# Where the layer norm's rows are kept between the norm and its transposition

## The chip, the core and the metric

The kernel runs on one core of one Trainium2 chip. A core has five engines that run their own instruction queues in order: TensorE (PE; its weight loads are shown apart as PEld), VectorE (DVE), ScalarE (ACT), GpSimd (POOL) and SyncE (SP), which here issues the DMA transfers. They wait for one another by semaphores. The metric is the device time of one execution in microseconds, the median of the runs.

## The reference, cut

Four batches of 768 tokens and 384 features pass through a gated linear attention scan, a Fourier mixer with a layer norm and an MLP, and a second mixer with an MLP over tokens and one over features.

```python
for t in range(S):                      # attention, per head, S = 768
    S_re, S_im = ar * S_re - ai * S_im + kv, ar * S_im + ai * S_re
    y[:, :, t] = np.einsum('bhd,bhde->bhe', q[:, :, t], S_re)
...
X = np.fft.fft(np.fft.fft(x, axis=1), axis=2)
u = x + np.real(X)
mu, var = mean(u), mean((u - mu) ** 2)
un = (u - mu) / np.sqrt(var + 1e-06)    # the layer norm
x = u + np.maximum(un @ w_ch1, 0.0) @ w_ch2
...
u = x + (np.maximum(x.T @ w_tok1, 0.0) @ w_tok2).T
out = u + np.maximum(u @ w_ch1, 0.0) @ w_ch2
```

## The kernel before

Work comes in two streams. The **chain** of a batch is stage 1 (a scan over 48 steps on DVE with its preparation on ACT and POOL, whose results PE transposes into a tile `qkt`, L642, and then eight chunks of attention: scores L753, L768/L769, outputs L802/L808) and stage 2 (the Fourier mixer: sums on DVE and POOL, L982, L988, L999; products L1022 and L1033; joins L1085 that give six tiles `u`; statistics L1092/L1093; the norm, L1112 on ACT and L1114 on DVE). The **dense** stream of a batch is a token mixing (L1147, L1165) between two MLPs (L926 into the hidden layer, L942 out of it). A dense product is a matmul of 128x128 by 128x384; they come in groups of nine that share a PSUM tile `l` of three, and each group ends in a DVE or ACT instruction that empties it (L930/L932 for `h`, L945 for `u`). Each layer works in quarters: 54 products of L926, then 54 of L942.

The chain of batch b+1 runs while the dense stream of batch b is worked off. Instructions get a priority from their stream and their place in the program, and a scheduler with a timeline of its own writes each engine's queue from it before the kernel runs; the order on the chip is then fixed. On PE the chain has priority over dense products, on DVE and ACT dense work has priority.

`transposed` (L900 to L911) takes the six normalized tiles in the order 0, 3, 1, 4, 2, 5: three transpositions on PE each (L906), a copy to `th` on ACT (L909) and the rest to `tl` on DVE (L910). `th` and `tl` are the inputs of the first MLP. Tiles come from pools: tag `qk` has one buffer of 12,288 words, used in turn as `qkt` in stage 1 and as the workspace `ws` in stage 2, with the layout `WSP`; tag `P` has two buffers of 384 words, used by `V` (L741), the values of an attention chunk. A tile's buffer is given to the next tile of its tag when all readers are done. The normalized rows `un` are the words 6176 to 8480 of `ws`, so that the next batch's `qkt` can't be written before L906 has read them.

A handover, below, is the place where the norm of a batch ends and its dense stream may begin. The first is that of batch 0, the fourth that of batch 3, after which only dense work is left. The last stage is stage 2 of batch 3.

Of the kernel before, what the change touches and what calls it, by code (L numbers as in the profile page):

```python
# [12 lines left out]
ACTF = mybir.ActivationFunctionType  # L13
ALU = mybir.AluOpType
# [22 lines left out]
OFF = ((2, 3), 1, 0)  # L37
# [16 lines left out]
def attn_fft_mixer_kernel(ctx: ExitStack, tc: tile.TileContext, aL, xL, vL, wL, qN, kN, vN, arN, aiN,  # L54
# [18 lines left out]
    ve, se, ge = Prio(nc.vector, "v"), Prio(nc.scalar, "v"), Prio(nc.gpsimd, "v")  # L73
# [11 lines left out]
    def shaped(v, shape):  # L85
        if len(shape) == 3:
            return v.rearrange("p (a b) -> p a b", b=shape[2])
        if len(shape) == 4:
            return v.rearrange("p (a b c) -> p a b c", b=shape[2], c=shape[3])
        return v  # L90

    def alloc(tag, shape, dt=F32, name=None):
        n = 1
        for x in shape[1:]:
            n *= x
        t = pool.tile([128, SIZE[tag]], dt, tag=tag, bufs=BUFS[tag], name=name or tag)
        return shaped(t[0:shape[0], 0:n], shape)
# [3 lines left out]
    def palloc(tag, shape):  # L101
        n = 1
        for s in shape[1:]:
            n *= s
        t = psum.tile([128, 512], F32, tag=tag, bufs=PSB[tag], name=tag)
        v = t[0:shape[0], 0:n]
        if len(shape) == 3:
            v = v.rearrange("p (a b) -> p a b", b=shape[2])
        return v

    def r32(ap):
        return ap.bitcast(F32)
# [46 lines left out]
    LAST = [None]  # L159
# [739 lines left out]
    def transposed(u, un, pt):  # L899
        th = [alloc("T", [128, 3, 384], F32R, name="th") for _ in range(2)]  # L900
        tl = [alloc("T", [128, 3, 384], F32R, name="tl") for _ in range(2)]
        for i in range(6) if un is None else (0, 3, 1, 4, 2, 5):
            src = u[i] if un is None else un[:, i, :]
            px = palloc(pt, [128, 3, 128])
            for dt in range(3):
                te.transpose(px[:, dt, :], src[:, dt * 128:dt * 128 + 128], ident)  # L906
            o = (i % 3) * 128
            hi = th[i // 3][:, :, o:o + 128]
            se.copy(out=hi, in_=px)  # L909
            ve.tensor_tensor(out=tl[i // 3][:, :, o:o + 128], in0=px, in1=r32(hi), op=ALU.subtract)  # L910
        return th, tl  # L911

    def mlp(u, b, p0, th, tl, done):
        for qd in range(4):
# [33 lines left out]


    WSP = {"xf": (0, 3072), "Z": (0, 1552), "xr": (1552, 1536), "fd": (3088, 3088), "cb": (3088, 1737),  # L950
           "xd": (6176, 3072), "un": (6176, 2304), "smat": (9248, 2048), "cc": (4825, 1158)}
    ZK = ((128, 64), (128, 64), (128, 65), (128, 63))

    def stage2(b):
        space = alloc("qk", [128, 12288], name="ws")
        def part(name, pat=None, **kw):
            o, n = WSP[name]
            v = space[:, o:o + n]
            return v.rearrange(pat, **kw) if pat else v

        smat = part("smat", "p (t k j) -> p t k j", t=4, k=2)
        sp.dma_start(out=smat, in_=cS)
        u = [alloc("u", [128, 384], name=f"u{i}") for i in range(6)]


        if b == 0:

            xm, xp = (alloc("h", [112, 4, 384], name="xf") for _ in range(2))
            xd = alloc("h", [112, 4, 384], name="xd")
            xd = [[xd[:, 0:2], xd[:, 2:4]], [alloc("tmp", [112, 2, 384], name="xd") for _ in range(2)]]  # L970
        else:
            xf = part("xf", "p (a b) -> p a b", a=8)[0:112]
            xm, xp = xf[:, 0:4, :], xf[:, 4:8, :]
            xd = part("xd", "p (s r a b) -> p s r a b", s=2, r=2, a=2)[0:112]
            xd = [[xd[:, s, r] for r in range(2)] for s in range(2)]
# [54 lines left out]
        def smm(o, ty, j0, first, last, extra=False):  # L1030
            for kt in range(2):
                kk = ZK[ty][kt]
                te.matmul(out=o, lhsT=smat[0:kk, ty, kt, j0:j0 + 128], rhs=Z[0:kk, 2 * ty + kt, 0:193],  # L1033
                          start=(first and kt == 0), stop=(last and kt == 1))
                if extra and kt == 0:
                    for k2 in range(2):
                        kk = ZK[2][k2]
                        te.matmul(out=o[0:1], lhsT=fk[0:kk, k2:k2 + 1], rhs=Z[0:kk, 4 + k2, 0:193], start=False, stop=False)
# [5 lines left out]
        def toks(i, dt):  # L1044
            x = xT if i < 3 else xr
            if i % 3 == 0:
                return x[:, dt, 1:257:2]
            if i % 3 == 1:
                return x[:, dt, 256:384]
            return x[:, dt, 0:256:2]  # L1050

        st = alloc("st", [128, 6, 6], name="bst")
        mv = alloc("st", [128, 6, 2], name="mv")
        rs = alloc("st", [128, 3, 2, 2], name="rs")
        un = part("un", "p (a b) -> p a b", a=6)
        for i in range(3):
            ps = palloc("s", [128, 2, 193])
            for pq in range(2):
                if i == 0:
                    smm(ps[:, pq, :], pq, 0, True, True)  # L1060
                elif i == 1:
                    smm(ps[:, pq, :], pq, 128, True, False)
                    smm(ps[:, pq, :], 2 + pq, 128, False, True)
                else:
                    smm(ps[:, pq, :], 2 + pq, 0, True, True, extra=(pq == 1))
            cb = part("cb", "p (i a b) -> p i a b", i=3, a=3)[:, i]
            if OFF[1]:
                cc = part("cc", "p (i a b) -> p i a b", i=3, a=2)[:, i]
                se.copy(out=cc, in_=ps)
                ge.tensor_tensor(out=cb[:, 1, :], in0=cc[:, 0, :], in1=cc[:, 1, :], op=ALU.subtract)  # L1070
                ge.tensor_tensor(out=cb[:, 2, :], in0=cc[:, 0, :], in1=cc[:, 1, :], op=ALU.add)
            else:
                se.copy(out=cb[:, 0, :], in_=ps[:, 1, :])
                ve.tensor_tensor(out=cb[:, 1, :], in0=ps[:, 0, :], in1=cb[:, 0, :], op=ALU.subtract)
                ve.tensor_tensor(out=cb[:, 2, :], in0=ps[:, 0, :], in1=cb[:, 0, :], op=ALU.add)
            for half in range(2):
                ti = i + 3 * half
                px = palloc("s", [128, 4, 112])
                for dt in range(4):
                    te.transpose(px[:, dt, :], toks(ti, dt), ident[0:112, 0:112])  # L1080

                def join(rows, o, c):
                    c = cb[0:rows, c, 0:193]
                    c = with_ap(c, 0, [(96, 2), (48, 2), (1, 48)]) if o == 0 else with_ap(c, 192, [(-96, 2), (-48, 2), (-1, 48)])
                    ve.tensor_tensor(out=with_ap(u[ti][0:rows], 192 * o, [(96, 2), (48, 2), (1, 48)]),  # L1085
                                     in0=with_ap(px[0:rows], 224 * o, [(112, 2), (64, 2), (1, 48)]), in1=c, op=ALU.add)
                lo, hi = (1, 2) if half == 0 else (2, 1)
                join(128, 0, lo)
                join(128, 1, hi)
                if i == 2:  # L1090
                    join(1, 1, lo)
                ve.bn_stats(out=st[:, ti, :], in_=u[ti])  # L1092
                ve.bn_aggr(out=mv[:, ti, :], in_=st[:, ti, :])  # L1093

            if b == 0 and i == 2:
                warm(16, ident)


            var = with_ap(mv, 2 * i + 1, [(6, 2)])
            w, y = rs[:, i, 0, :], rs[:, i, 1, :]  # L1100
            se.activation(out=w, in_=var, func=ACTF.Ln, bias=eps)
            se.activation(out=y, in_=w, func=ACTF.Exp, scale=-0.5)
            mean = with_ap(mv, 2 * i, [(6, 2)])
            ve.tensor_tensor(out=w, in0=y, in1=y, op=ALU.mult)
            ve.scalar_tensor_tensor(out=w, in0=var, scalar=1e-6, in1=w, op0=ALU.add, op1=ALU.mult)
            ve.tensor_scalar(out=w, in0=w, scalar1=-0.5, scalar2=1.5, op0=ALU.mult, op1=ALU.add)
            ve.tensor_tensor(out=y, in0=y, in1=w, op=ALU.mult)
            ve.scalar_tensor_tensor(out=w, in0=mean, scalar=-1.0, in1=y, op0=ALU.mult, op1=ALU.mult)
            for half in range(2):
                ti = i + 3 * half  # L1110
                if OFF[0][b > 0] >> half & 1:
                    LAST[0] = se.activation(out=un[:, ti, :], in_=u[ti], func=ACTF.Identity, scale=y[:, half:half + 1], bias=w[:, half:half + 1])  # L1112
                else:
                    LAST[0] = ve.tensor_scalar(out=un[:, ti, :], in0=u[ti], scalar1=mv[:, ti, 0:1], scalar2=y[:, half:half + 1],  # L1114
                                 op0=ALU.subtract, op1=ALU.mult)

        return u, un


    def go(g, n=99):  # L1120
# [74 lines left out]
    def on(s, f, *args):  # L1195
        stream[0] = s
        return f(*args)
# [7 lines left out]
    u, norm = on(FIRST, chain, 0)  # L1205
    t1 = on(FIRST, transposed, u, norm, "s")
    feed(56)
    for b in range(B - 2):
# [8 lines left out]
        u = u1  # L1217
# [12 lines left out]
    with tc.If(fv != 0):  # L1230
        with tc.For_i(0, B, 1) as b:
            fallback(b)
            u, norm = stage2(B)
# [113 lines left out]
```

## Time and profile before

| | |
|---|---|
| median of 3 runs | 1102.39 us (1101.18 to 1103.57) |
| the profiled execution | 1103.4 us, of it 1101.6 us span |
| PE busy | 985.5 us, 89% of the span |
| DVE busy | 784.3 us, 71% |
| ACT busy | 506.2 us, 46% |
| POOL busy | 387.3 us, 35% |
| granted TensorE clock, mean | 0.955 |

The span runs from the first instruction to the last; the profiled execution took 1.8 us more than its span. A busy share is a mean over stages: the first 190 us belong to the scan of batch 0, in which PE has little to do, and the last 260 us to dense products alone.

### The profile page before, as it was taken

The page shows a single profiled execution, that of the slowest core. Times are in us where ns is not written, and L with a number is a line of the kernel's source. Part 1 is how long each engine was busy: PE and PEld are TensorE (multiplying, and loading weights), DVE is VectorE, ACT ScalarE, POOL GpSimd, SP SyncE. Part 2 cuts the span into 40 slices and gives each one's busy share as a digit, 9 for nine tenths or more (in the row PEclk, how much of TensorE's full clock was granted, in tenths as well). Part 3 has the DMA queues.
Part 4 walks back from the last instruction along what each step waited for, and adds up shares of the span by engine and source line. Part 5 has one row for each costly group of instructions (what it writes and reads, how often), then busy time and mean ns, then how long its engine had stood idle before and what let it go on. Part 6 is the DMA issues. An engine that isn't in the chain of part 4 may idle for free.

```text
span 1101.6 us, 21033 instructions
## 1 busy us (share of the span) xinstructions
PE 985.5 (89%) x7314; PEld 923.1 (84%) x7314; DVE 784.3 (71%) x2115; ACT 506.2 (46%) x1393; POOL 387.3 (35%) x520
## 2 busy tenths in 40 slices
PE   1368887999889999799998999999986999999997
PEld 0237775989788888699998899999976999999997
DVE  6986987999999668999767879985555433433332
ACT  6753355777876225867423567751124112121111
POOL 6643985573576444223226312211432002000000
PEclk9987797999999998899998999999988999999999
DMA  6137954686758664355565336655412433443432
GB/s 215 45 82 179 293 176 154 209 283 194 231 179 278 194 178 135 99 168 185 179 160 172 112 112 193 205 161 146 139 48 66 151 115 129 158 151 130 165 101 74
DMA packets 101536, 174.65 MB, mean 159 GB/s; under 512 B 11056, under 2 KB 61104, under 8 KB 100912
## 3 DMA queue, kind: packets, MB, share of 16 engines
q1 hardware_dynamic: 101424, 173.24, 51.1%
q8 instruction: 60, 0.98, 0.4%
q14 instruction: 52, 0.43, 0.1%
HBM read 133.88 MB, written 39.32 MB: 157 GB/s over the span
## 4 chain that ended last, share of the span: by engine, by line
PE 65%; DVE 10%; DMA 2%; ACT 1%; issue 1%; POOL 1%; SPq 0%; POOLq 0%; DVEq 0%; ACTq 0%
PE l L942 24%; PE l L926 22%; PE s L753 3%; PE s L642 2%; PE s L1033 2%; PE s L1022 2%; PE s L802 2%; DMA cvt<-wL 2%; PE s L808 1%; PE s L1147 1%; DVE ws L982 1%; PE s L1165 1%; PE s L768 1%; DVE cvt L199 1%; PE s L906 1%
## 5 line engine op out<-in xcount | busy, mean ns | idle before, releaser
L942 PE MATMUL l<-w,h 128*128 128x384 f32 x1728 | 332.5, 345 | 12.1 <-DVE h L932 8.4
L926 PE MATMUL l<-th,w 128*128 128x384 f32 x1152 | 314.4, 342 | 5.1 <-DVE h L932 2.6
L942 PEld LDWEIGHTS l<-w,h 128*128 128x128 f32 x1728 | 304.4, 192 | 16.8 <-DVE h L932 11.6
L926 PEld LDWEIGHTS l<-th,w 128*128 128x128 f32 x1152 | 210.8, 190 | 9.1 <-DVE h L932 4.1
L930 ACT ACTIVATE h<-l 128x384 fp32r<-128x384 f32 x192 | 94.0, 490 | 225.3 <-PE l L926 224.8
L926 PE MATMUL l<-tl,w 128*128 128x384 f32 x576 | 195.3, 339 | 0.0
L932 DVE SCALAR_TENSOR_TENSOR h<-l,h 128x384 fp32r<-128x384 f32 x192 | 106.2, 553 | 88.3 <-ACT h L930 87.9
L945 DVE TENSOR_TENSOR u<-u,l 128x384 f32<-128x384 f32 x192 | 105.4, 550 | 76.0 <-PE l L942 75.1
L926 PEld LDWEIGHTS l<-tl,w 128*128 128x128 f32 x576 | 109.1, 189 | 0.4 <-issue 0.2
L196 POOL TENSOR_TENSOR cvt<-cvt 128x384 int32<-128x384 int32 x56 | 64.8, 1163 | 38.2 <-DVE cvt L194 9.4
L466 PE MATMUL s<-misc,y 128*112 128x128 f32 x96 | 22.1, 377 | 52.1 <-DVE y L444 48.6
L753 PE MATMUL s<-qkt 112*96 112x96 f32 x512 | 59.7, 267 | 8.0 <-DVE sc L760 7.9
L466 PEld LDWEIGHTS s<-misc,y 128*112 128x112 f32 x96 | 14.5, 181 | 61.9 <-issue 27.3
L753 PEld LDWEIGHTS s<-qkt 112*96 112x96 f32 x512 | 53.4, 177 | 11.1 <-DVE sc L760 8.7
L786 POOL TENSOR_TENSOR yc<-Aa,gm 48x384 f32<-48x384 f32 x18 | 21.0, 1165 | 100.8 <-DVE Aa L779 100.8
L206 POOL TENSOR_TENSOR w<-cvt,w 128x384 fp32r<-128x384 f32 x44 | 51.1, 1170 | 10.5 <-ACT w L205 7.0
L199 DVE SCALAR_TENSOR_TENSOR cvt<-cvt 128x384 int32<-128x384 int32 x56 | 48.8, 878 | 7.0 <-POOL cvt L196 6.8
L1132 POOL TENSOR_TENSOR xl<-u,xh 128x384 fp32r<-128x384 f32 x18 | 17.9, 1004 | 101.1 <-ACT xh L1131 101.1
L571 POOL TENSOR_TENSOR tm<-tm 128x144 f32<-128x144 f32 (+1 forms) x51 | 26.6, 523 | 73.7 <-ACT tm L570 73.7
L642 PE MATMUL s<-misc,y 128*112 128x128 f32 x288 | 45.7, 275 | 1.5 <-DVE y L626 1.0
L615 DVE TENSOR_TENSOR p<-p,A 128x144 f32<-128x144 f32 x144 | 44.7, 310 | 2.0
L589 POOL TENSOR_TENSOR A<-raw,tm 128x144 f32<-128x144 f32 (+1 forms) x51 | 26.1, 513 | 56.0 <-DVE tm L587 29.4
(232 smaller groups left out, 1905.3 us busy)
## 6 DMA issues: line engine op xcount, KB each, us to landing
w<-wscr SPq DMA_DIRECT2D x180, 384.0 KB, 3.5
cvt<-wL SPq DMA_DIRECT2D x56, 384.0 KB, 4.7
wscr<-w SPq DMA_DIRECT2D x44, 384.0 KB, 3.2
Kn<-kn SPq DMA_DIRECT2D x64, 192.0 KB, 3.8
kn<-y SPq DMA_DIRECT2D x96, 96.0 KB, 2.7
raw<-aL SPq DMA_DIRECT2D x48, 144.0 KB, 3.0
xx<-xL SPq DMA_DIRECT2D x48, 144.0 KB, 3.2
V<-vL SPq DMA_DIRECT2D x32, 144.0 KB, 3.3
```

Of the source, the lines that this page charges most:

```text
L196: x = ge.tensor_tensor(out=a, in0=a, in1=lo, op=ALU.add)
L199: rest(ve.scalar_tensor_tensor(out=a, in0=hi, scalar=-0x80000000, in1=a, op0=ALU.bitwise_and, op1=ALU.bitwise_or))
L206: ge.tensor_tensor(out=parts[:, 1, :], in0=a.bitcast(F32), in1=r32(parts[:, 0, :]), op=ALU.subtract)
L466: te.transpose(ps[:, j, :], y[:, j, 0:112], ident)
L615: ve.tensor_tensor(out=cur, in0=prev, in1=A[:, j, 0:3, :], op=ALU.mult)
L642: te.transpose(ps[:, j, :], y[:, j, 0:112], ident)
L753: te.matmul(out=ps[:, j, :], lhsT=K[:, hc, :], rhs=Q[:, hc, :])
L926: te.matmul(out=ps, lhsT=w1[:, wi, kt * 128:kt * 128 + 128], rhs=x[g][:, kt, :], start=(n == 0), stop=(n == 8))
L930: x = se.activation(out=hi, in_=ps, func=ACTF.Relu)
L932: ve.scalar_tensor_tensor(out=h[:, 1, g * 384:g * 384 + 384], in0=ps, scalar=0.0, in1=r32(hi), op0=ALU.max, op1=ALU.subtract)
L942: te.matmul(out=ps, lhsT=hs[m][:, hi, tt * 128:tt * 128 + 128], rhs=w2[:, wi, :], start=(n == 0), stop=(n == 8))
L945: ve.tensor_tensor(out=u[tt], in0=u[tt], in1=ps, op=ALU.add)
```

## The change

The norm is no longer written in stage 2. Stage 2 keeps, for each tile, what the norm needs (scale, bias, mean and which engine), and hands back a function; `transposed` calls it just ahead of a tile's transposition, and it writes one of the two buffers of tag `P`. The region `un` leaves the workspace. The instructions are as many as before.

```diff
         for i in range(6) if un is None else (0, 3, 1, 4, 2, 5):
-            src = u[i] if un is None else un[:, i, :]
+            src = u[i] if un is None else un(i)
             px = palloc(pt, [128, 3, 128])
...
-           "xd": (6176, 3072), "un": (6176, 2304), "smat": (9248, 2048), "cc": (4825, 1158)}
+           "xd": (6176, 3072), "smat": (9248, 2048), "cc": (4825, 1158)}
...
-        un = part("un", "p (a b) -> p a b", a=6)
+        norms = {}
...
             for half in range(2):
-                ti = i + 3 * half
-                if OFF[0][b > 0] >> half & 1:
-                    LAST[0] = se.activation(out=un[:, ti, :], in_=u[ti], func=ACTF.Identity, scale=y[:, half:half + 1], bias=w[:, half:half + 1])
-                else:
-                    LAST[0] = ve.tensor_scalar(out=un[:, ti, :], in0=u[ti], scalar1=mv[:, ti, 0:1], scalar2=y[:, half:half + 1],
-                                 op0=ALU.subtract, op1=ALU.mult)
-
-        return u, un
+                norms[i + 3 * half] = (y[:, half:half + 1], w[:, half:half + 1], mv[:, i + 3 * half, 0:1], OFF[0][b > 0] >> half & 1)
+
+        def normalized(ti):
+
+            y, w, mean, on_act = norms[ti]
+            un = alloc("P", [128, 384], name="un")
+            if on_act:
+                LAST[0] = se.activation(out=un, in_=u[ti], func=ACTF.Identity, scale=y, bias=w)
+            else:
+                LAST[0] = ve.tensor_scalar(out=un, in0=u[ti], scalar1=mean, scalar2=y, op0=ALU.subtract, op1=ALU.mult)
+            return un
+
+        return u, normalized
```

The scheduler writes other queues for the changed program. Lines behind the norm have numbers that are higher by 5 in it; L1117 is the norm on ACT (L1112 before).

On PE, at the end of stage 1 of batch 2, the last outputs L808 are followed by what is left of the quarter of L926 (`x` counts equal rows). Before:

```order
L808 MATMUL s<-qkt,T 64x96
L808 MATMUL s<-qkt,T 48x96
L926 MATMUL l<-th,w 128x384
L926 MATMUL l<-tl,w 128x384
L926 MATMUL l<-th,w 128x384 x2
L926 MATMUL l<-tl,w 128x384
...
L926 MATMUL l<-th,w 128x384
L942 MATMUL l<-w,h 128x384 x18
L1022 MATMUL s<-dcos,ws 128x97 x4
```

After:

```order
L808 MATMUL s<-qkt,T 64x96
L808 MATMUL s<-qkt,T 48x96
L942 MATMUL l<-w,h 128x384 x45
L1022 MATMUL s<-dcos,ws 128x97 x5
L942 MATMUL l<-w,h 128x384 x9
L1022 MATMUL s<-dcos,ws 128x97 x3
```

Before, 21 products of L926 stood behind the last L808 here; now none does, and all 54 stand ahead of it.

On PE, in the last stage, the last L808 of batch 3 is followed by the last dense products that can run before the norm. Before:

```order
L808 MATMUL s<-qkt,T 48x96
L942 MATMUL l<-w,h 128x384 x45
L1022 MATMUL s<-dcos,ws 128x97 x12
L942 MATMUL l<-w,h 128x384 x9
L1022 MATMUL s<-dcos,ws 128x97 x4
```

After:

```order
L808 MATMUL s<-qkt,T 48x96
L942 MATMUL l<-w,h 128x384 x31
L1022 MATMUL s<-dcos,ws 128x97 x16
L1022 MATMUL s<-dcos,ws 64x97 x8
L1022 MATMUL s<-dcos,ws 65x97 x4
```

Of 54 dense products behind that L808, 31 are left there; 23 now stand ahead of it, and none stands among L1022.

On ACT, at the second handover, the norms of batch 1 (tiles `u`), the copies L909 and the scan of batch 2 (L567 to L593, L558) stand among one another. Before:

```order
L1102 ACTIVATE rs<-rs 128x2
L1112 ACTIVATE ws<-u_3214,rs 128x384
L1112 ACTIVATE ws<-u_3217,rs 128x384
L570 ACTIVATE tm<-tm 128x144
L909 CAST th<-s 128x3x128
L1112 ACTIVATE ws<-u_3215,rs 128x384
L1112 ACTIVATE ws<-u_3218,rs 128x384
L909 CAST th<-s 128x3x128
L578 ACTIVATE tm<-tm 128x144
L592 ACTIVATE A<-tm 128x3x48
L909 CAST th<-s 128x3x128 x2
```

After:

```order
L1117 ACTIVATE un<-u_3220,rs 128x384
L1117 ACTIVATE un<-u_3223,rs 128x384
L578 ACTIVATE tm<-tm 128x144
L909 CAST th<-s 128x3x128
L1117 ACTIVATE un<-u_3221,rs 128x384
L592 ACTIVATE A<-tm 128x3x48
L909 CAST th<-s 128x3x128
L1117 ACTIVATE un<-u_3224,rs 128x384
L590 COPY A<-A 128x3x48
L593 ACTIVATE A<-A 128x3x48
L558 ACTIVATE sq<-raw 128x288
L909 CAST th<-s 128x3x128 x2
```

The last two norms no longer stand together, and L590, L593 and L558 of the scan now stand between the last norm and the last two copies.

## Rows read from the trace of the kernel before

**Rows 1.** The page's head: busy us, share of the span, instructions.

```profile
span 1101.6 us, 21033 instructions
PE 985.5 (89%) x7314; PEld 923.1 (84%) x7314; DVE 784.3 (71%) x2115; ACT 506.2 (46%) x1393; POOL 387.3 (35%) x520
```

**Rows 2.** Busy time by stretch: us, busy (instructions) per engine, granted clock, DMA.

```profile
core 0: us, PE busy (x) PEld busy (x) DVE busy (x) ACT busy (x) POOL busy (x), PEclk, DMA share, GB/s
200.00:220.00 20.00, 18.78 (x108) 17.40 (x107) 19.82 (x53) 14.60 (x41) 12.57 (x15) 1.00 0.70 226
...
640.00:740.00 100.00, 100.00 (x615) 98.94 (x614) 87.16 (x288) 64.73 (x190) 20.70 (x47) 1.00 0.58 175
795.00:810.00 15.00, 11.58 (x55) 11.26 (x54) 15.00 (x18) 3.14 (x11) 10.32 (x6) 0.77 0.20 71
...
841.00:1102.00 261.00, 254.74 (x1477) 254.14 (x1475) 95.75 (x174) 45.90 (x95) 6.08 (x6) 0.99 0.40 131
```

**Rows 3.** The chain that ended last, in order of time: start, us, what.

```profile
794.90 4.31 DVE ws L982 x2
...
803.08 6.03 PE l L942 x18
809.11 2.65 PE s L1022 x24
811.76 1.59 PE l L942 x9
813.35 3.97 PE s L1022 x40
...
839.50 1.54 PE s L906 x6
...
1058.29 9.36 PE l L926 x54
```

**Rows 4.** Timeline, second handover: start, us, engine, line, instruction [idle before, releaser].

```profile
443.89 0.60 DVE L1085 TENSOR_TENSOR u<-s,ws 1x192 f32<-1x192 f32 x2
...
449.82 1.31 ACT L1112 ACTIVATE ws<-u,rs 128x384 f32<-128x384 f32 x2
...
450.58 1.54 PE L906 MATMUL s<-misc,ws 128*128 128x128 f32 x6 [0.53 <-ACT ws L1112]
...
452.13 0.89 PE L642 MATMUL s<-misc,y 128*112 128x128 f32 x3
452.67 1.31 PE L926 MATMUL l<-th,w 128*128 128x384 f32 x3
452.90 0.31 ACT L590 COPY A<-A 128x144 f32<-128x144 f32 x1 [0.23 <-POOL A L589]
453.49 0.32 ACT L593 ACTIVATE A<-A 128x144 f32<-128x144 f32 x1
453.72 0.43 ACT L558 ACTIVATE sq<-raw 128x288 f32<-128x288 f32 x1
```

**Rows 5.** Stage 1 of batches 2 and 3 on PE: L753's first and last start.

```profile
L753 PE MATMUL s<-qkt x128: 246/248/324, 546.0 to 586.2; 112*96 112x96 f32 x128
L753 PE MATMUL s<-qkt x128: 246/248/324, 748.8 to 790.1; 112*96 112x96 f32 x128
```

**Rows 6.** Timeline of PE: a run of plain transpositions, and the ends of both stages 1.

```profile
568.57 1.15 PE L906 MATMUL l<-misc,u 128*128 128x128 f32 x9
590.52 0.34 PE L808 MATMUL s<-qkt,T 112*48 112x96 f32 x4
794.44 0.34 PE L808 MATMUL s<-qkt,T 112*48 112x96 f32 x4
```

**Rows 7.** Timeline of ACT at the first handover: a conversion's two instructions, the last norm.

```profile
182.41 0.53 ACT L191 ACTIVATE cvt<-cvt 128x384 f32<-128x384 f32 x1
182.84 0.52 ACT L192 ACTIVATE cvt<-cvt 128x384 int32<-128x384 uint32 x1
183.56 0.71 ACT L1112 ACTIVATE ws<-u,rs 128x384 f32<-128x384 f32 x1 [0.19 <-DVE rs L1108]
```

## The prediction

> **What bounds the kernel now.** I read the page's head first [rows 1]: PE is busy 985.5 us of 1101.6, so its work is the floor, and a change is worth what it adds to or takes from PE's idle and slow stretches. The busy time by stretch says where those lie [rows 2]. From 841 us on only dense products are left: 254.7 of 261 us busy, at full clock. This tail is the same work whatever comes before, so the end moves as the fourth handover moves, one for one. Between 200 and 220 us DVE is busy 19.8 of 20 us, and the scan of batch 1 goes at its pace. At 640 to 740 us PE is busy throughout. At 795 to 810 PE is busy 11.6 of 15 us at a mean clock of 0.77.
>
> The chain that ended last [rows 3] shows why: the long DVE sums of the last stage (L982 from 794.90), a few dense products beside them, L1022, L1033, the last transpositions of the norm (L906, 839.50 to 841.04), then nothing but dense work. So from 795 to 841 the chain alone sets the end, and dense products do no more than lie beside it; before that PE's queue sets it.
>
> That stage 1 goes at the pace of PE's queue I take from two batches. Batch 2's runs from 546.0 [rows 5] to 590.86 (590.52 and 0.34, [rows 6]): 44.9 us. Batch 3's runs from 748.8 to 794.78: 46.0 us. In the queues' order 69 dense products and 18 transpositions of `u` stand in the first, 90 products in the second. A product is 9.36 / 54 = 0.173 us [rows 3], a transposition 1.15 / 9 = 0.128 us [rows 6]. So the second should be longer by 21 x 0.173 - 18 x 0.128 = 1.3 us, and it is by 1.1. What stands in PE's queue there is paid for in full.
>
> **The change, part by part.** Six norms and 18 transpositions a batch stay as they are, at the same shapes; nothing is added or removed, so busy time stays. What moves is a release, a buffer, and the order of the queues.
>
> *The workspace is free earlier.* Its last reader now is the join at 444.49 (443.89 and 0.60) and no longer the transposition at 452.12 (450.58 and 1.54), 7.6 us later [rows 4]. The scan of batch 2 needs `qkt` for L642. But L642 stands behind the 18 L906 in PE's queue at the second handover, after the change too, and begins at 452.13; at the third it stands behind the last L906 as well. A queue that runs in order gives the release nothing: 0, with a gain of 7.6 us as the far bound.
>
> *Two buffers.* The third tile's norm waits for the first tile's transposition. The norms come in pairs, and a pair is transposed before the next one's data are there: L906 of a pair ends within 1.54 us, the pairs' statistics are further apart. This alone: 0. But the norm now has the place of `transposed` in the program, behind its rivals on ACT. At the second handover L590, L593 and L558 stand between the last norm and the last two copies, for which the first L926 waits at 452.67: 0.31 + 0.32 + 0.43 = 1.06 us [rows 4]. Bounds: 0, if they find a gap while ACT waits for PE; 2.1 us, if the norm slips by as much again. PE has no dense work left there, so nothing covers it. I take 1.1. At the first handover one more conversion (L191 and L192, 0.53 + 0.52 us) stands ahead of the last norm at 183.56 [rows 7]. Bounds 0 and 1.1; since that conversion has to be done anyway, and DVE is the limit right after, I take half, 0.5. The loads of `V` share the pool and now wait for L906 in SP's queue; behind them is L630, whose `y` comes only after L642, so 0.
>
> *Dense products move ahead of the chain.* This is the large term. Behind the last L808 of batch 2 stood 21 products of the quarter of L926; now none does, so 21 more are worked off in front of it. For batch 3, 31 of 54 are left, so 23 stand ahead. Stage 1 pays for them in full, as the two batches showed: 23 x 0.173 = 4.0 us by which the last stage begins later. The products are not lost, but where they stood they lay beside DVE's L982 to L999, in time that PE had to wait through anyway. Bounds: 4.0, and 0 if PE finds time for them between chunks.
>
> *The last stage gets shorter.* Nine of the products stood between L1022: 1.59 us at 811.76 [rows 3], right on the chain. They are gone from there: -1.6. L1022 also followed 18 products that took 6.03 us from 803.08; with those ahead it could start when DVE and ACT are ready, perhaps 1.6 us sooner, but DVE now has three L945 ahead of L999 where it had two. So the gain's bound is -3.2, and I count only -1.6. The other bound: PE now sits idle longer before L1022. The 18 products took 0.335 us each in the stretch with a clock of 0.77, behind a wait, against 0.173 at full clock: a factor of 1.93. If the first 24 records of L1022 (2.65 us) paid it, that is 2.5 us more: +0.9.
>
> The Trainium skill ("TensorE: Matmul & The Clock Gate", Part 1: The HAM clock gate) speaks against this change: products behind an idle stretch run at 1.2 GHz and not 2.4. By that rule the last stage gives back its gain and the sum below is 6.5 in place of 4.0. The trace agrees on the size with its 1.93 for the 18 products; it doesn't show how long a wait before L1022 will be.
>
> **Sum:** 0 + 0.5 + 1.1 + 4.0 - 1.6 = +4.0 us. On the profiled execution this is a span of 1105.6, with the 1.8 us around it 1107.4. That execution lies 1.0 above the median shown, so I forecast a median of 1106.4. The measurement tells 0.2%, 2.2 us, from no change.
>
> **The rivals.**
> 1. *The freed workspace pays (faster).* The scan of the next batch starts its transpositions up to 7.6 us earlier at a handover, and the chain ends earlier. For it: the hold is there in the trace, at every handover. Against it: L642 stays behind L906 in the queue. It decides from 6.2 us on, since the 4.0 have to be made good and 2.2 won; with all of it, 4.0 - 7.6 = -3.6, 1098.8 us. The Trainium skill ("Perfetto Trace Analysis", Optimization Strategy) reads a gap that repeats on the engine that should be saturated as a sign of too few buffers for the next tile; by it, this is the likely outcome. Here the gaps before L906 are ended by ACT's norm, not by a buffer, as the row at 450.58 shows. Chance 0.16.
> 2. *Hidden (no change).* Stage 1 has slack between chunks, since "busy" on PE isn't PE at its peak, and takes in most of the 21 products; or PE loses less in the last stage, where it waited 3.4 us (795.00 to 810.00, 11.58 busy). Then what is left is 0.5 + 1.1 - 1.6 = 0: 1102.4 us. Against it: 1.3 us worked out against 1.1 measured. Chance 0.24.
> 3. *The low clock in the last stage (slower still).* 4.0 + 2.5 = 6.5: 1108.9 us. Chance 0.12.
>
> My forecast has 0.48. With the third rival, slower has 0.60, the second is "same", 0.24, the first "faster", 0.16. The forecast's own range is 1104.6 to 1108.5. To leave no more than 2 in 10 out, it reaches down into the first rival, to 1100.0, and up past the third, to 1110.0, where late norms of 2.1 and 1.1 us would meet the low clock.
>
> **What the profile after would show.** PE's busy time as before, within a few us. L906 of batch 1 ending 1 to 2 us later than 452.1, with ACT ahead of the L926 behind it. Stage 1 of batch 2 at some 48.5 us in place of 44.9. The last L808 some 5.6 us later than 794.78, and from there to the last L906 about 44.7 us in place of 46.3. The tail unchanged at 261 us. The forecast is wrong if stage 1 of batch 2 stays at 45 us with more products in it (rival 2), if L642 of batch 2 starts before 450 us (rival 1), or if the scan of batch 1, whose rows on DVE, POOL and SP change places in many spots, ends more than 2 us off: that I have not costed, since counts on DVE differ by two instructions at its end.

## The result and the profile after

The changed kernel takes 1110.45 us (median of 5 runs, 1108.14 to 1112.21), the kernel before on the same chip 1103.43 (5 runs, 1101.18 to 1103.69): a ratio of 1.0068, interval 1.0055 to 1.0082. It is slower by 7.0 us, where 4.0 were forecast; 1110.45 lies 0.45 above the range. The forecast counted from 1102.39, the median of three runs; five give 1103.43, 1.0 more, so that the 7.0 against 4.0 says more than the 0.45.

The head of the page of the changed kernel, against [rows 1]:

```profile
span 1109.3 us, 21041 instructions
PE 982.7 (89%) x7314; PEld 917.8 (83%) x7314; DVE 786.8 (71%) x2115; ACT 501.8 (45%) x1393; POOL 386.9 (35%) x520
```

The instruction counts (x) of the engines are those of before. PE is busy 2.8 us less and DVE 2.5 us more. With a span 7.7 us longer, PE is without work for 126.6 us, where it was 116.1.

Busy time by stretch, changed kernel: a busy stretch of the middle, the last stage in four pieces, its slow part in finer ones, the tail.

```profile
core 0: us, PE busy (x) PEld busy (x) DVE busy (x) ACT busy (x) POOL busy (x), PEclk, DMA share, GB/s
640.00:740.00 100.00, 100.00 (x615) 97.96 (x614) 87.70 (x295) 64.56 (x193) 22.46 (x51) 1.00 0.55 169
...
800.00:806.00 6.00, 5.25 (x52) 4.81 (x48) 4.64 (x3) 1.12 (x2) 4.57 (x2) 1.00 0.45 175
806.00:814.00 8.00, 1.89 (x10) 1.57 (x10) 8.00 (x11) 1.92 (x5) 5.48 (x5) 0.96 0.42 147
814.00:820.00 6.00, 6.00 (x28) 6.00 (x29) 2.46 (x6) 1.85 (x9) 0.00 (x0) 0.50 0.01 3
820.00:826.00 6.00, 6.00 (x41) 5.22 (x40) 0.00 (x0) 1.65 (x5) 0.00 (x0) 0.70 0.00 0
...
814.00:823.00 9.00, 9.00 (x44) 8.83 (x45) 2.46 (x6) 2.51 (x11) 0.00 (x0) 0.50 0.01 2
823.00:824.00 1.00, 1.00 (x9) 0.86 (x8) 0.00 (x0) 0.18 (x1) 0.00 (x0) 0.72 0.00 0
824.00:826.00 2.00, 2.00 (x19) 1.53 (x17) 0.00 (x0) 0.81 (x3) 0.00 (x0) 1.00 0.00 0
...
849.00:1109.00 260.00, 254.73 (x1477) 254.13 (x1476) 95.77 (x174) 45.98 (x96) 6.09 (x6) 0.99 0.40 131
```

The tail is the same work in the same time as in [rows 2] (254.73 us busy against 254.74), so the loss is complete when the last L906 ends. From 806 to 814 PE has 1.89 us of work. After that it runs at a granted clock of 0.50, the level of 1.2 GHz, up to about 823, and at 1.00 from 824 on. Some 45 of the 64 records of L1022 fall into the slow part.

The chain that ended last, in order of time, against [rows 3]:

```profile
801.36 4.31 DVE ws L982 x2
...
806.13 4.64 DVE ws L988 x4
...
813.95 11.46 PE s L1022 x64
...
847.65 1.54 PE s L906 x6
```

Before, the 64 records of L1022 took 2.65 + 3.97 = 6.62 us, with nine dense products between them. Now the nine are gone, and the same 64 take 11.46. The timeline of PE has what stood ahead of them:

```profile
806.19 1.84 PE L942 MATMUL l<-w,h 128*128 128x384 f32 x9 [0.94 <-DVE u L945]
813.95 11.46 PE L1022 MATMUL s<-dcos,ws 112*128 112x97 f32 x64 [5.92 <-ACT ws L1006]
```

In the kernel before, busy time by stretch around the 18 dense products (803.08 to 809.11) and the first L1022, with the clock in the same column:

```profile
805.00:809.00 4.00, 4.00 (x15) 4.00 (x14) 4.00 (x9) 2.73 (x10) 1.25 (x1) 0.52 0.00 0
809.00:812.00 3.00, 3.00 (x28) 3.00 (x27) 1.77 (x4) 0.77 (x3) 0.00 (x0) 1.00 0.02 5
```

There the slow stretch, 0.52, fell on the dense products, and L1022 began at 1.00.

Stage 1 of batch 2 on PE, L753 and L808 by first and last start, against [rows 5, 6]:

```profile
L753 PE MATMUL s<-qkt x128: 246/248/323, 550.2 to 594.0; 112*96 112x96 f32 x128
...
L808 PE MATMUL s<-qkt,T x112: 243/245/248, 565.1 to 598.4; 112*48 112x96 f32 x56, 112*64 112x96 f32 x56
```

From the first L753 to the last L808 it is 48.2 us, where [rows 5, 6] give 590.6 - 546.0 = 44.6, on the same starts: 3.6 more, as 21 products of 0.173 us would have it. (The 48.5 of the prediction counts to the end of the last L808.)

The second handover, timelines of ACT and PE in the changed kernel, against [rows 4] (L1117 is the norm):

```profile
451.54 1.31 ACT L1117 ACTIVATE un<-u,rs 128x384 f32<-128x384 f32 x2 [0.60 <-DVE rs L1108]
...
453.61 0.71 ACT L1117 ACTIVATE un<-u,rs 128x384 f32<-128x384 f32 x1
454.23 0.31 ACT L592 ACTIVATE A<-tm 128x144 f32<-128x144 f32 x1
454.44 0.47 ACT L909 CAST th<-s 128x384 fp32r<-128x384 f32 x1
454.80 0.71 ACT L1117 ACTIVATE un<-u,rs 128x384 f32<-128x384 f32 x1
...
456.16 0.84 ACT L909 CAST th<-s 128x384 fp32r<-128x384 f32 x2
```

```profile
454.38 0.90 PE L906 MATMUL s<-misc,un 128*128 128x128 f32 x3 [0.53 <-ACT un L1117]
455.56 0.90 PE L906 MATMUL s<-misc,un 128*128 128x128 f32 x3 [0.28 <-ACT un L1117]
456.25 0.85 PE L642 MATMUL s<-misc,y 128*112 128x128 f32 x3
456.75 1.31 PE L926 MATMUL l<-th,w 128*128 128x384 f32 x3
```

The last two norms are no longer a pair: a copy L909 and a piece of the next scan stand between them. They take from 453.61 to 455.51, 1.90 us where a pair takes 1.31, and L906 follows in two halves.

### The profile page after: what moved, and what is told of

Its sections match the earlier page's. It is cut to its first block, busy times and chain, and to the rows that moved or that the text cites. A ratio compares the mean times of both kernels' runs of the same rounds, so it can differ in the third digit from the quotient of the medians.

```text
span 1109.3 us, 21041 instructions
## 1 busy us (share of the span) xinstructions
PE 982.7 (89%) x7314; PEld 917.8 (83%) x7314; DVE 786.8 (71%) x2115; ACT 501.8 (45%) x1393; POOL 386.9 (35%) x520
## 4 chain that ended last, share of the span: by engine, by line
PE 67%; DVE 17%; DMA 5%; POOL 4%; ACT 4%; issue 2%; SPq 1%; POOLq 0%; DVEq 0%; ACTq 0%
PE l L926 23%; PE l L942 22%; PE s L753 4%; PE s L642 2%; PE s L1033 2%; DVE cvt L199 2%; PE s L1022 2%; PE s L802 2%; DVE ws L988 1%; DMA Kn<-kn 1%; PE s L808 1%; PE s L1152 1%; DVE ws L982 1%; PE s L1170 1%; PE l L1170 1%
## 5 line engine op out<-in xcount | busy, mean ns | idle before, releaser
L942 PE MATMUL l<-w,h 128*128 128x384 f32 x1728 | 324.1, 339 | 11.8 <-DVE u L945 7.5
L926 PE MATMUL l<-th,w 128*128 128x384 f32 x1152 | 315.4, 342 | 7.2 <-DVE h L932 4.5
L942 PEld LDWEIGHTS l<-w,h 128*128 128x128 f32 x1728 | 297.7, 188 | 16.9 <-DVE u L945 9.6
L926 PEld LDWEIGHTS l<-th,w 128*128 128x128 f32 x1152 | 210.3, 189 | 11.2 <-DVE h L932 6.5
L926 PE MATMUL l<-tl,w 128*128 128x384 f32 x576 | 194.9, 338 | 0.0
L926 PEld LDWEIGHTS l<-tl,w 128*128 128x128 f32 x576 | 108.9, 189 | 0.4 <-DVE tl L910 0.3
L753 PE MATMUL s<-qkt 112*96 112x96 f32 x512 | 59.8, 266 | 9.0 <-DVE sc L760 9.0
L753 PEld LDWEIGHTS s<-qkt 112*96 112x96 f32 x512 | 53.2, 175 | 12.0 <-DVE sc L760 10.0
L206 POOL TENSOR_TENSOR w<-cvt,w 128x384 fp32r<-128x384 f32 x44 | 51.5, 1178 | 9.4 <-ACT w L205 5.6
L642 PE MATMUL s<-misc,y 128*112 128x128 f32 x288 | 45.8, 277 | 0.5 <-DVE y L626 0.4
L615 DVE TENSOR_TENSOR p<-p,A 128x144 f32<-128x144 f32 x144 | 44.6, 310 | 2.0
```

The costliest lines, as they stand in the source:

```text
L206: ge.tensor_tensor(out=parts[:, 1, :], in0=a.bitcast(F32), in1=r32(parts[:, 0, :]), op=ALU.subtract)
L615: ve.tensor_tensor(out=cur, in0=prev, in1=A[:, j, 0:3, :], op=ALU.mult)
L642: te.transpose(ps[:, j, :], y[:, j, 0:112], ident)
L753: te.matmul(out=ps[:, j, :], lhsT=K[:, hc, :], rhs=Q[:, hc, :])
L926: te.matmul(out=ps, lhsT=w1[:, wi, kt * 128:kt * 128 + 128], rhs=x[g][:, kt, :], start=(n == 0), stop=(n == 8))
L942: te.matmul(out=ps, lhsT=hs[m][:, hi, tt * 128:tt * 128 + 128], rhs=w2[:, wi, :], start=(n == 0), stop=(n == 8))
```

## The experiments

Each kernel was timed beside the kernel before, on the same chip; "ahead" is the number of dense products in PE's queue ahead of the last L808 of batches 2 and 3. "Stage 1" is batch 2 from the first L753 to the last L808, "last stage" batch 3 from the last L808 to the last L906, both by the starts in each profiled execution. The starts are rounded to 0.1 us, so that a difference of 0.1 between two rows means nothing.

| kernel | median us (runs) | ratio to before | ahead | stage 1 | last stage |
|---|---|---|---|---|---|
| before | 1103.43 (5) | | 1473, 2250 | 44.6 | 46.1 |
| after | 1110.45 (5) | 1.0068 [1.0055, 1.0082] | 1494, 2273 | 48.2 | 47.8 |
| e1 late place, workspace | 1103.12 (11) | 1.0 [0.9991, 1.0008] | 1473, 2250 | 44.5 | 46.1 |
| e2 batch 0 alone changed | 1109.71 (6) | 1.006 [1.0044, 1.0077] | 1494, 2271 | 48.3 | 48.1 |
| e3 batches 1 to 3 changed | 1103.94 (11) | 1.0001 [0.9985, 1.0017] | 1473, 2242 | 44.6 | 47.1 |
| e4 after, seven products | 1113.52 (5) | 1.0087 [1.0073, 1.0101] | 1494, 2273 | 48.3 | 51.5 |
| e5 after, 3 + 18 products | 1108.52 (5) | 1.0045 [1.0032, 1.0059] | 1494, 2273 | 48.2 | 46.1 |
| e6 two buffers, old priority | 1102.99 (11) | 1.0004 [0.9994, 1.0014] | 1473, 2242 | 44.6 | 47.7 |
| e7 three buffers | 1107.63 (6) | 1.0052 [1.0035, 1.0068] | 1494, 2271 | 48.0 | 48.1 |
| e8 before, nine products | 1105.49 (11) | 1.0014 [1.0002, 1.0026] | 1473, 2250 | 44.6 | 46.1 |
| e9 after, 2 + 12 products | 1105.87 (11) | 1.0021 [1.0011, 1.0031] | 1494, 2273 | 48.3 | 43.7 |
| e10 e6, eight products | 1103.7 (12) | 1.0009 [0.9997, 1.0022] | 1473, 2242 | 44.6 | 47.9 |

**The late place without the buffers.** The norm is called from `transposed`, as in the change, but writes to the workspace, as before:

```diff
+        rows = part("un", "p (a b) -> p a b", a=6)
...
-            un = alloc("P", [128, 384], name="un")
+            un = rows[:, ti, :]
```

> The norm is called from the transposition as in the change, but writes its old region of the workspace. If the two buffers cause the loss (my theory: the third tile's norm has to wait for the first tile's transposition, and the queues are written around that wait), this is near the kernel before: 1103 to 1105 us, stage 1 of batch 2 at some 45 us, the last L808 within 1.5 us of 794.8. If the norm's later place in the program causes it (rival), it is near the changed kernel: 1109 to 1111 us, last L808 near 801.

1103.12 us, no change. The later place in the program alone costs nothing.

**Batch 0 alone, and all but batch 0.** A flag per batch chooses between the norm as before and as in the change:

```diff
+        early = b != 0        # e3: b == 0
+        rows = part("un", "p (a b) -> p a b", a=6) if early else None
...
+            return norms[ti] if early else norm(ti, alloc("P", [128, 384], name="un"))
```

> The change for batch 0 alone; batches 1 to 3 keep their rows in the workspace. My theory: the loss begins at the first handover (last L906 2.2 us later, first L753 of batch 1 4.1 us later) and the order of later queues follows from it, so this has nearly all of it: 1109 to 1111 us. Rival: each handover loses its share by its own buffers, then this has a third or less of it: 1104 to 1106 us.

> The change for batches 1 to 3 alone; batch 0 keeps its rows in the workspace. My theory: near the kernel before, 1102 to 1105 us. Rival (each handover loses its share): 1107 to 1110 us.

1109.71 and 1103.94 us. Nearly all of the loss comes with the norm of batch 0, hundreds of microseconds ahead of where it shows: stage 1 of batch 2 is at 48.3 us, and in the last stage the 64 records of L1022 take 11.88 us. Batches 1 to 3 alone cost nothing that the interval shows. There, and with the old priority below, eight dense products that stood ahead of the last L808 of batch 3 stand behind it (2242), with 18 among L1022 and not nine. The last stage is 1.0 and 1.6 us longer, and the median doesn't show it: eight products fewer ahead of the last stage are 8 x 0.173 = 1.4 us. So the length of the last stage alone is no price; it counts together with what stands ahead of it.

**Seven plain products in the last stage.** Products on the sums, one on L982, two on L988 and four on L999, to keep PE at work; their results are not used:

```diff
...
-                    if b == 0 and ty < 2:
-                        warm(1, fd[:, ty, r, 0, 1:191])
+                    if b in (0, 3) and ty < 2:
+                        warm(1, fd[:, ty, r, 0, 1:191], "s" if b else "l")
```

> The changed kernel with seven plain products into an unused PSUM tile in the last stage, each behind one of the sums of L982, L988 and L999, so that PE isn't idle for 5.9 us ahead of L1022. They compute nothing that is used. If the low clock costs what the trace shows (64 L1022 in 11.5 us against 6.6 before), this is faster than the changed kernel by 3 to 4.5 us: 1106 to 1107.5 us. Rival: the chain waits for DVE's joins anyway and the seven products only add work: within 1 us of 1110.4.

1113.52 us, 3 us slower than the changed kernel, against the theory. The timeline of PE says why this doesn't refute it (a plain product shows as two records here):

```profile
804.42 2.05 PE L942 MATMUL l<-w,h 128*128 128x384 f32 x9
808.02 0.88 PE L309 MATMUL s<-ws,misc 112*128 112x384 f32 x2 [1.55 <-DVE ws L988]
809.10 1.62 PE L309 MATMUL s<-ws,misc 112*128 112x384 f32 x2 [0.19 <-DVE ws L988]
811.99 3.17 PE L309 MATMUL s<-ws,misc 112*128 112x190 f32 x8 [1.28 <-DVE ws L999]
814.95 12.06 PE L1022 MATMUL s<-dcos,ws 112*128 112x97 f32 x64
```

PE still waited 1.55 and 1.28 us, and the second product on L988 already takes twice as long as the first (1.62 against 0.88): the clock had fallen. Busy time by stretch has it at 0.50 from 810 us on:

```profile
810.00:815.00 5.00, 3.72 (x11) 2.61 (x10) 4.64 (x10) 2.73 (x10) 1.00 (x1) 0.50 0.01 5
```

The last four read `fd`, into which L1006 writes on ACT, so that L1006 had to wait for them (twice 0.46 us), and L1022 begins 15.8 us behind the last L808 and not 12.9. The run tells nothing on the price of the clock.

**A filling without gaps.** Plain products on the first part of L982 and of L988 alone, which nothing writes afterwards before L1022: three where PE waits ahead of the nine dense products, 18 behind them.

```diff
+                if b == 3 and k + s == 0:
+                    warm(3, xm[:, 0, 0:288], "s")
...
+                    if b == 3 and k + s + r == 0:
+                        warm(18, xd[0][0][:, 0, 0:288], "s")
```

> The changed kernel, with 21 plain products (112x128 by 112x288, results not used) in the last stage, between the sums L982/L988 and L1022: three where PE waits 0.94 us ahead of the nine products, and 18 behind these, of which 18 x 0.33 us at full clock fill the 5.9 us before L1022. None reads or writes what L1006 or L999 write. Theory (the clock): the 64 records of L1022 took 11.46 us after against 2.65 + 3.97 before because PE had sat idle; filled, they take 6.6 to 7 us, from the last L808 to the last L906 it is 43 us and not 47.8, and the median is 1105.0 to 1106.5. Rival (the clock falls in spite of the filling, as with the seven products, or is not the price): L1022 stays near 11.4 us, the 18 take up to 12, and the median is 1110 to 1116.

1108.52 us, 1.9 less than the changed kernel, with 21 products more. The price of a filling product was expected at 0.33 us and is 0.494 (8.89 / 18), so the filling ended late. Timeline of PE (L1026 is L1022):

```profile
806.34 1.97 PE L942 MATMUL l<-w,h 128*128 128x384 f32 x9
808.14 8.89 PE L309 MATMUL s<-ws,misc 112*128 112x288 f32 x36
816.87 6.81 PE L1026 MATMUL s<-dcos,ws 112*128 112x97 f32 x64
```

Both executions have the last L808 at 801.0. L1022 begins 2.9 us later than in the changed kernel, takes 6.81 us and not 11.46, and ends 1.7 us sooner. The size of the median was missed (1105.0 to 1106.5); the clock as its cause is shown. The next run shortened the filling to the wait.

**The filling as long as the wait.** Two products and 12; the edit is against the run above.

```diff
-                    warm(3, xm[:, 0, 0:288], "s")
+                    warm(2, xm[:, 0, 0:288], "s")
...
-                        warm(18, xd[0][0][:, 0, 0:288], "s")
+                        warm(12, xd[0][0][:, 0, 0:288], "s")
```

> The changed kernel with the filling of the first kind made shorter: two such products ahead of the nine, and 12 behind them (in the run with 18 those took 8.89 us, 0.494 each, so that L1022 began 2.9 us later than in the changed kernel, though its 64 records took 6.81 us and not 11.46). Twelve take 5.9 us, as long as PE waited. Theory (the clock): L1022 begins 12.9 us behind the last L808, as in the changed kernel, and takes 6.8 us; from the last L808 to the last L906 43.2 us in place of 47.8, the median 1105.0 to 1106.5. Rival (a filling of that length isn't enough to hold the clock): L1022 near 11 us, 1110.

1105.87 us, inside the interval of the theory: 4.6 us less than the changed kernel. Timeline of PE:

```profile
808.09 1.85 PE L942 MATMUL l<-w,h 128*128 128x384 f32 x9
809.78 5.98 PE L309 MATMUL s<-ws,misc 112*128 112x288 f32 x24
815.85 0.69 PE L1026 MATMUL s<-dcos,ws 112*128 112x97 f32 x4
816.78 6.47 PE L1026 MATMUL s<-dcos,ws 112*128 112x97 f32 x60 [0.24 <-ACT ws L1010]
```

And its busy time by stretch:

```profile
806.00:814.00 8.00, 8.00 (x38) 6.57 (x37) 8.00 (x9) 0.08 (x1) 6.39 (x5) 1.00 0.61 220
814.00:820.00 6.00, 5.67 (x40) 4.77 (x38) 4.36 (x9) 3.70 (x13) 1.00 (x1) 1.00 0.01 4
```

The clock is 1.00 where it was 0.50, and the last stage takes 43.7 us in place of 47.8 (43.2 were expected). The 64 records take 7.40 us, from 815.85 to 823.25, with a wait of 0.24 us for ACT among them.

**Two buffers with the old priority.** The buffers of the change, but the norm is issued with the priority that it had in stage 2:

```diff
...
+            tc.cur_priority = rank
             if on_act:
-                LAST[0] = se.activation(out=un, in_=u[ti], func=ACTF.Identity, scale=y, bias=w)
+                LAST[0] = nc.scalar.activation(out=un, in_=u[ti], func=ACTF.Identity, scale=y, bias=w)
...
```

> The changed kernel with its two buffers, but each norm issued with the priority that it had in stage 2. In PE's queue the dense products then stand as before at stage 1 of batch 2 (1473 ahead of its last L808, after: 1494) and nearly so at batch 3 (2242 against 2250). Theory (the order of the dense products is what costs): 1102.5 to 1104.5, as before. Rival (two buffers make the norm wait for its transposition): 1108 to 1111, as after, with ACT's norm held by L906.

1102.99 us. Two buffers cost nothing where the dense products stand as before at stage 1 of batch 2, and nearly so at batch 3.

**Three buffers.**

```diff
-    BUFS = {"e": 10, "A": 2, "tmp": 2, "P": 2, "qk": 1,
+    BUFS = {"e": 10, "A": 2, "tmp": 2, "P": 3, "qk": 1,
```

> The changed kernel with three buffers in the pool in place of two; PE's queue has 1494 dense products ahead of the last L808 of batch 2, as after, and 2271 ahead of batch 3's. Theory (the order): stage 1 of batch 2 at 48 us, L1022 of the last stage near 11.4 us, 1108.5 to 1111. Rival (a wait for one of two buffers costs): that wait is gone, 1103 to 1105.

1107.63 us: slower than before with a buffer more, with stage 1 at 48.0 us and L1022 at 11.89. It misses the expected interval by 0.9, on the low side. PE's queue differs from that of the change elsewhere too (774 dense products ahead of the first L753 of batch 1, not 780), and its execution reaches that L753 at 354.4 us and not at 360.3; whether the third buffer has a part in these 2.8 us stays open. A wait for one of two buffers shows nowhere in the changed kernel: DVE never sits idle ahead of its norms (L1119), and those on ACT have one line among the waits of the whole execution (us in total, times, longest):

```profile
ACT un L1117 <- DVE rs L1108: 3.1, 4, 1.7
```

These are waits for the statistics. From the first L753 of batch 1 to the last L808 of batch 3 the kernel with three takes 442.5 us, the changed program 440.7 to 443.2 in four executions (its own and those of the three runs with products in the last stage): no gain from the third buffer shows there.

**Fillings in kernels with the old order.** Nine products in the kernel before, eight in the one with the old priority, where PE waits 3.42 and 4.25 us ahead of 18 slow products.

```diff
+                if b == 3 and k + s == 0:
+                    warm(9, xm[:, 0, 0:288], "s")
```

> The kernel before with nine such products (results not used) where PE waits 3.42 us ahead of the 18 slow products in the last stage; the scheduler then puts 13, not 18, ahead of L1022. Theory (the clock falls in that wait and the 18 products pay 6.03 us in place of 3.1, beside DVE's sums): L1022 can begin 1 to 2 us sooner, until L999 on DVE and L1006 on ACT hold it, 1101.5 to 1103. Rival (DVE's sums set L1022's start anyway, so that the slow products cost nothing): 1103 to 1104.5.

> Two buffers with the norm's old priority (1102.99 us), and eight such products where PE waited 4.25 us ahead of 18 slow products in the last stage. Theory (the slow products, 4.97 us in place of 3.1, hold L1022 back): L1022 begins up to 1 us sooner, 1101.5 to 1103. Rival (they lie beside DVE's sums, and the scheduler's other order of the dense products among L1022 takes the rest): 1103 to 1105, as in the kernel before with a filling (1105.49).

1105.49 and 1103.7 us: no gain, as the rivals had it, and the first lies 1.0 above even theirs. In the first, L1022 did begin sooner, 13.0 us behind the last L808 and not 14.4, and then waited for ACT. But the scheduler put 14 dense products among L1022 where there had been nine, and the last stage stayed at 46.1 us. Its rise by 1.4 thousandths isn't explained by the last stage, and is left open. No version tried beats the kernel before.

## Why the prediction was wrong

**The step that failed is the term of the last stage, and in it the price of the low clock.** The term was put at -1.6, with +0.9 as its dear end, and measured +1.7 (47.8 against 46.1 us). The gain that it counted came: the nine products are gone from between L1022. So did the one that it left as a bound: L1022 begins 12.9 us behind the last L808 where it began 14.4. With the clock held, in the run of the filling as long as the wait, the stage took 43.7 us, where the prediction had 44.7 for it. What failed is the price of the clock. The sum put it at nothing, and its dear end went no further than "If the first 24 records of L1022 (2.65 us) paid it, that is 2.5 us more". Some 45 of the 64 records paid it, and the price was 47.8 - 43.7 = 4.1 us by the filled run, or 11.46 - 6.62 = 4.84 us against the records of the kernel before.

In the kernel before, PE ran 18 products slowly from 803.08 to 809.11, beside DVE's sums, and the clock was at 1.00 behind them. In the changed kernel 23 dense products have moved away from there, the waiting stretch lies bare, and L1022 takes over the slow part, on the chain. It also stays slow for longer, over 9 us of L1022 where it was some 6 us of dense products; the prediction's 24 records would have been 2.65 x 1.93 = 5.1 us. Rival 3 is what happened, at 1.6 to 2 times its price. The Trainium skill ("TensorE: Matmul & The Clock Gate", Part 1: The HAM clock gate) has products behind an idle stretch run at the lower level, and the trace agrees: 0.50 granted behind 5.92 us of waiting, 1.00 where the wait is filled.

The range also stops short of the prediction's own terms: late norms of 2.1 and 1.1 us, the 4.0 and the dear end of 0.9 are 8.1 us, 1110.5, and not 1110.0.

**The dense products ahead of the chain, +4.0: right.** Stage 1 of batch 2 was forecast at +3.6 for its 21 products, and six kernels with 1494 ahead have 48.0 to 48.3 us, six with 1473 have 44.5 to 44.6. The two products of batch 3 don't show: from the last L808 of batch 2 to that of batch 3 the mean of the changed program (four executions: its own and those of the three runs with products in the last stage, which differ from it only there) is 203.3 us, against 204.1 in two executions of the program before (the second is that with nine products). The four themselves are 202.6 twice and 204.0 twice, so the 0.8 between the means can't be put down to the change. Counted with it the term came to +2.9.

**The first handover, +0.5: too small, within the scatter.** The profiled execution of the changed kernel reaches the first L753 of batch 1 4.1 us later than that of before, which alone would meet the prediction's last sign (the scan of batch 1 more than 2 us off). The four executions stand at 357.6 to 360.3 us there, the two of before at 356.2 and 358.3; the means differ by 1.6. One execution of each can't tell a cost of 2 us here.

**The second handover, +1.1: not told from the scatter, and not by its cause.** From that L753 to the last L906 of batch 1 the means differ by 0.55 us, from there to the first L753 of batch 2 by 0.4; the two executions of the program before differ by 0.7 themselves in the first of these. L590, L593 and L558 do stand ahead of the last copies, but beside the last L906, for which the last copy waits anyway; L926 follows the first L642 by 0.50 us, in [rows 4] by 0.54. What the timeline shows in their place is the pair taken apart, 1.90 - 1.31 = 0.6 us; no run has tested it alone. "The norms come in pairs" was read from the order of before.

**The terms at nothing: right.** L642 of batch 2 begins at 456.25 us, behind L906, so the earlier release of the workspace gave nothing, and rival 1 fell. Two buffers alone cost nothing, and no norm waited for one. The rule of rival 1 in the Trainium skill ("Perfetto Trace Analysis", Optimization Strategy), by which a gap that repeats can mean too few buffers, finds no support here: the freed workspace gave nothing, and with three buffers the kernel is still slower than before.

Up to the last L808 the sum was +5.6; measured are +6.5 in the profiled execution and +5.5 in the means (1.6 + 0.55 + 0.4 + 2.9). With +1.7 for the last stage and the tail at 260.5 us against 261.0, the profiled execution comes to its +7.7. Had the last stage come out as forecast, 3.3 us shorter, the median would have been about 1107.1, inside the range.

That the order of the dense products turns on batch 0's norm, and neither on its late place alone nor on its buffers alone, is shown by the runs (1473 products ahead of the last L808 of batch 2 with either alone, 1494 with both for batch 0). Why the scheduler then writes another order for batch 2 stays open.

## What to carry to other kernels

Where a scheduler writes the queues, the price of a change to a buffer lies in the new order, perhaps two batches later: read which work moved past which wait, and price it at both ends. Work that lies in a wait of TensorE can be free there and still spare what follows on the chain the low clock (4.1 us here); when it moves away, price the run behind the wait at the low level, and not its first records alone. Compare lengths of stages, over several executions of one program, rather than times since the start: here those differed by 2.7 us at the first L753 of batch 1 already.

## What was not expected of the hardware

Seven products with waits of 0.56, 1.55, 0.19 and 1.28 us ahead of and among them didn't hold the clock: it was 0.50 from 810 to 815 us, and L1022 behind them took 12.06 us. Fourteen without a wait, two ahead of nine dense products and 12 behind them, held it at 1.00.

How long the low clock lasted wasn't the same for all work: behind 3.42 us of waiting it was back at 1.00 after some 6 us of dense products (kernel before), behind 5.92 us of waiting after more than 9 us of L1022 (changed kernel), with PE busy throughout in both.

A filling of useless work made the changed kernel faster: 14 plain products more, and 4.6 us less.
